# Retention and a GELU feed-forward on one core: the second batch by chunk, weight sums on VectorE, queries in token order, tails among other loads, and later chunks spread over seven blocks

## Chip, core and metric

One core of a Trainium2 chip. The metric is the device time of one execution in microseconds (us); the profile of one execution is taken on the chip beside the timed runs.

## What is computed

`q`, `k`, `v` are float32 of shape (8 batches, 8 heads, 576 tokens, 64). Each head has a decay; the attention has no softmax. Its output, laid out as 4608 tokens x 512, goes through a feed-forward with a tanh GELU.

```python
scores = scale * np.matmul(q, k.transpose(0, 1, 3, 2))
gamma = 1.0 - 2.0 ** (-5.0 - np.arange(H))
Dmat = np.where(rel >= 0, gamma[:, None, None] ** rel[None, :, :], 0.0)   # rel = query position - key position
attn = np.matmul(scores * Dmat, v)
x = attn.transpose(0, 2, 1, 3).reshape(4608, 512)
h = x @ w_in                                                             # 512 x 2048
out = gelu_tanh(h) @ w_out                                               # 2048 x 512
```

## The kernel before

*Attention.* A batch is cut into four chunks of 128 tokens (`c` = 0 to 3) and a tail of 64 (`c` = 4, called `NC`). The decay is split into factors on q and k, so that casting q and k from float32 to float16 also multiplies by a table `sc`. For each chunk:

- `cast` turns loaded float32 (`ld`, 16 buffers; `lt`, 3 buffers for tails) into `cq`, `ck`, `cv`;
- `turn_pe` and `turn_tail` transpose q and k on TensorE (PE) and copy the result to `tq` and `tk`; batches 4 to 7 use a DMA transpose instead (`turn_dma`, issued from ScalarE's queue);
- `score` multiplies keys by queries into two PSUM banks, and VectorE masks them (`ret`);
- `state` makes the chunk's 64x64 state, `scan` adds it to the running state on VectorE (`ws`) and spreads it into a block-diagonal tile (`tbd`);
- `av` makes the chunk's output from `ret`, v and the state of the chunk before, and `put` copies it from PSUM to `xT` on ScalarE (ACT). `xT` is a ring of 1536 tokens.

q is loaded in another order than k and v: a partition holds four neighbouring tokens, in pieces of 1 KB, where k and v come in pieces of 256 bytes. So `tq` and the scores have the tokens of a chunk in an interleaved order, and `put` undoes it with a strided write (`i j` to `j i`).

*Feed-forward.* Tokens go in nine tiles of 512; what runs for tile `t` is called block `t`. `up(t, fc)` makes one of 16 slices of h (four matmuls of 512 columns) and ACT applies the GELU into `gT`. Block 0's second product is plain (64 matmuls, two in each of 32 steps, with a store step behind each 16). Blocks 1 to 8 use a seven-product scheme with half-size operands: `act_sums` adds and subtracts quarters of `gT` on VectorE, `weight_sums` does so once for w_out, and `prod(t, m, u)` runs products m = 1, 6, 5, 7, 2, 3, 4 in two halves each; `after` combines the results and stores them. Such a block has 30 steps: 0 to 15 `up`, 16 to 29 `prod`.

*Order.* The order of work is written out by hand: `at(t, u, f)` hangs an attention piece on step u of block t, and engines work through their instructions in that order. Batch 0 runs first, beside the loads; up(0) follows with batch 0's tail between its slices (`late`); batch 1 hangs on block 0; batch b from 2 on hangs on block b-1, with five scores at steps 1, 7, 12, 19, 25 (6, 10, 15, 19, 25 for batch 2). Blocks 7 and 8 have no attention. POOL casts most q and k, ACT casts v.

All loads and stores are issued from SP, in one order, `seq`: batch 0 (q, then k and v by chunk, then tails), w_in, w_out, then batch by batch. `pump` issues the next load when a cast has freed an `ld` buffer.

Of the kernel before, what the change touches and what calls it, by code (L numbers as in the profile page):

```python
# [10 lines left out]
ALU = mybir.AluOpType  # L11
# [8 lines left out]
def kernel(  # L20
# [25 lines left out]
    QT = NC  # L46
    TB = 512
# [19 lines left out]
    def ldt():  # L67
        return sb.tile([128, 256], F32, tag="lt", name="lt", bufs=3)
# [4 lines left out]
    def load(b, key, c):  # L73
        src = SRC[key]
        if c == NC:
            t = ldt()
            for u in range(2):
                nc.sync.dma_start(  # L78
                    out=t[64 * u : 64 * u + 64, :].rearrange("p (h d) -> p h d", d=D),
                    in_=src[b, 4 * u : 4 * u + 4, M0:S, :].rearrange("h s d -> s h d"),  # L80
                )
        elif key == "q":
# [30 lines left out]
    for b in range(1, B):  # L113
        seq += [("b", b, "q", p) for p in range(HP)]
        seq += [("b", b, key, c) for c in range(NC) for key in "kv"]
        seq += [("b", b, key, NC) for key in "kqv"]
# [30 lines left out]
    NE = 8 + HP * 8 + 8  # L147
# [5 lines left out]
    for j in range(QT):  # L153
# [6 lines left out]
        )  # L160
    for u in range(2):
# [6 lines left out]
    nc.vector.tensor_scalar(out=sc[:, 8:44], in0=sc[:, 8:44], scalar1=scale, scalar2=None, op0=ALU.mult)  # L168
    warm = const.tile([128, 1], F32, name="warm")
# [6 lines left out]
    cm = const.tile([128, HP, QT, 32], F32, name="cm")  # L176
# [3 lines left out]
        pattern=[[0, HP], [1, QT], [QT, 32]], channel_multiplier=-1,  # L180
# [31 lines left out]
    def cast(b, key, c, eng):  # L212
# [9 lines left out]
        elif key == "q" and c < NC:  # L222
# [7 lines left out]
        else:  # L230
            s0, nh = (0, 8) if c < NC else ({"q": 40, "k": 44}[key], 4)
# [7 lines left out]
    def new_turned(b):  # L239
        a = att[b]  # L240
        for key in "kq":
            a["t" + key] = sb.tile([128, NB, 128], F16, tag="t" + key, name="t" + key, bufs=2)

    def turn_pe(b, key, c0, n, copy, tag="att"):
        a = att[b]
        t = bank(tag, "tr", F16)
        for i in range(n):
            nc.tensor.transpose(
                t[:, 128 * i : 128 * i + 128],
                a[key][:, 128 * (c0 + i) : 128 * (c0 + i) + 128],  # L250
                ident,
            )
# [463 lines left out]
```

## Time and profile before

| | |
|---|---|
| time, median of 3 runs | 345.28 us (344.16 to 345.38) |
| the profiled execution | 344.22 us; span 342.3 us from first to last instruction |
| busy, share of the span | PE 91%, DVE (VectorE) 62%, ACT 50%, POOL 32% |
| DMA | 51.30 MB, mean 150 GB/s |
| mean granted TensorE clock | 0.973 of full |

The span is cut into 40 equal slices. Each digit is the busy share of a slice in tenths; PEclk is the granted TensorE clock in tenths:

```profile
PE   5869849994697999999999999999999999999995
DVE  7751644879978467757976677467546752442432
ACT  3575516782455247525752673368326623613610
POOL 7748234999920460039224404100000000000000
PEclk9999969997889999999999999999999999999999
DMA  7979998989901999896986978410730003003003
```

One slice is 8.6 us. Batch 0 and up(0) take the first five, block 0 the next three and a half, block 1 the six behind those.

### The profile page before, as it was taken

Reading aid. Unit: us, or ns where it says so; the run is one execution under the profiler, and the core shown is the slowest. Engines: PE = TensorE matmul, PEld = TensorE weight load, DVE = VectorE, ACT = ScalarE, POOL = GpSimd, SP = SyncE. Lnnn points to the kernel's source line nnn. Section 1 sums busy time; section 2 is a strip of 40 time slices with the busy share of each in tenths; the row PEclk is TensorE's granted clock in tenths of the full one; section 3 lists DMA queues with packets and bytes.
Section 4 is the critical chain, followed back from the end, with each engine's and each line's share of the span. In section 5 each row is a group of like instructions: output and inputs, shape, how many; then the busy total and the mean of one; then the engine's idle time right before and its main releaser. Section 6 shows DMA issues by size and latency. Waiting matters only on the chain.

```text
span 342.3 us, 6651 instructions
## 1 busy us (share of the span) xinstructions
PE 310.2 (91%) x2660; PEld 189.1 (55%) x2660; DVE 213.1 (62%) x437; ACT 170.9 (50%) x274; POOL 108.8 (32%) x129
## 2 busy tenths in 40 slices
PE   5869849994697999999999999999999999999995
PEld 2434324452246854784477448745864585486484
DVE  7751644879978467757976677467546752442432
ACT  3575516782455247525752673368326623613610
POOL 7748234999920460039224404100000000000000
PEclk9999969997889999999999999999999999999999
DMA  7979998989901999896986978410730003003003
GB/s 204 194 204 359 388 288 178 247 169 296 207 6 31 229 188 293 166 188 205 256 170 159 283 162 101 139 39 2 138 124 0 2 2 123 0 2 123 2 0 124
DMA packets 116559, 51.30 MB, mean 150 GB/s; under 512 B 99632, under 2 KB 107824, under 8 KB 116528
## 3 DMA queue, kind: packets, MB, share of 16 engines
q1 hardware_dynamic: 97840, 46.15, 52.0%
q10 hardware_dynamic: 18688, 4.72, 8.1%
q8 instruction: 21, 0.34, 0.4%
q14 instruction: 10, 0.08, 0.1%
HBM read 36.70 MB, written 9.44 MB: 135 GB/s over the span
## 4 chain that ended last, share of the span: by engine, by line
PE 72%; DMA 8%; DVE 8%; SPq 5%; ACT 4%; issue 1%; POOL 1%; DVEq 0%
PE hp L390 30%; PE opB L466 12%; PE opC L466 9%; PE opA L466 8%; PE op L408 3%; DMA ld<-in_moe_w_in_dram 3%; DMA ld<-in_moe_w_out_dram 3%; PE xs L338 3%; SPq L90 3%; PE st L289 2%; PE xs L356 2%; ACT xT L377 2%; PE us L309 2%; DMA ld<-in_q_dram 2%; SPq L78 1%
## 5 line engine op out<-in xcount | busy, mean ns | idle before, releaser
L390 PE MATMUL hp<-xT,w_in_sb 128*128 128x512 f16 x576 | 136.3, 387 | 2.1 <-ACT xT L377 1.9
L396 ACT ACTIVATE gT<-hp 128x512 f16<-128x512 f32 x144 | 86.5, 605 | 67.7 <-PE hp L390 67.7
L390 PEld LDWEIGHTS <-w_in_sb 128*128 128x128 f16 x576 | 54.7, 99 | 63.3 <-issue 6.8
L298 DVE TENSOR_TENSOR ret<-st,cm 128x512 f16<-128x512 f32 x64 | 41.2, 685 | 27.5 <-PE st L289 27.5
L377 ACT CAST xT<-xs 128x512 f16<-128x512 f32 x31 | 40.1, 1294 | 29.5 <-PE xs L356 22.6
L466 PEld LDWEIGHTS <-gT 128*128 128x128 f16 x512 | 49.1, 98 | 6.5 <-issue 0.7
L223 POOL TENSOR_TENSOR cq<-ld,sc 128x512 f16<-128x512 f32 x28 | 31.6, 1155 | 46.0 <-DMA tq<-cq 21.0
L232 POOL TENSOR_TENSOR ck<-ld,sc 128x512 f16<-128x512 f32 x27 | 28.9, 1089 | 37.3 <-PE us L309 29.6
L466 PEld LDWEIGHTS <-s 128*128 128x128 f16 x384 | 36.5, 98 | 4.9
L466 PE MATMUL opA<-w_out_sb,gT 128*128 128x256 f16 x256 | 30.9, 273 | 0.0
L448 DVE TENSOR_TENSOR s<-gT 128x512 f16<-128x512 f16 x32 | 15.0, 469 | 21.5 <-ACT gT L396 21.1
L480 DVE TENSOR_TENSOR k<-k,opB 128x512 f32<-128x512 f32 x16 | 11.0, 687 | 23.7 <-PE opB L466 23.6
L289 PE MATMUL st<-tq,tk 64*128 64x128 f16 x288 | 15.8, 226 | 9.3 <-DVE tk L254 8.6
L329 DVE CAST tbd<-ws 64x256 f16<-64x256 f32 x48 | 20.6, 430 | 1.2
L289 PEld LDWEIGHTS <-tk 64*128 64x128 f16 x288 | 8.5, 96 | 22.9 <-DVE tk L254 11.1
L338 PEld LDWEIGHTS <-cv 128*64 128x64 f16 x288 | 9.6, 110 | 16.3 <-issue 13.9
L408 PE MATMUL op<-w_out_sb,gT 128*128 128x512 f16 x64 | 17.7, 396 | 0.5 <-ACT ost L413 0.5
L219 ACT CAST cv<-ld 128x512 f16<-128x512 f32 x28 | 17.5, 628 | 1.1 <-DMA ld<-in_v_dram 1.1
L480 DVE TENSOR_TENSOR ost<-k,opC 128x512 f32<-128x512 f32 x16 | 11.0, 687 | 11.0 <-PE opC L466 10.8
L338 PE MATMUL xs<-ret,cv 128*64 128x128 f16 x288 | 16.1, 228 | 1.1 <-ACT xT L377 1.1
L466 PE MATMUL opB<-wt,gT 128*128 128x256 f16 x128 | 16.4, 273 | 0.5 <-DVE ost L480 0.5
L449 DVE TENSOR_TENSOR s<-s,gT 128x512 f16<-128x512 f16 x32 | 15.9, 498 | 1.1
(92 smaller groups left out, 338.9 us busy)
## 6 DMA issues: line engine op xcount, KB each, us to landing
out_dram<-ost SPq DMA_DIRECT2D x17, 512.0 KB, 3.1
ld<-in_q_dram SPq DMA_DIRECT2D x32, 256.0 KB, 4.7
ld<-in_k_dram SPq DMA_DIRECT2D x32, 256.0 KB, 5.7
ld<-in_v_dram SPq DMA_DIRECT2D x32, 256.0 KB, 5.1
ld<-in_moe_w_in_dram SPq DMA_DIRECT2D x16, 256.0 KB, 6.2
ld<-in_moe_w_out_dram SPq DMA_DIRECT2D x16, 256.0 KB, 5.4
lt<-in_k_dram SPq DMA_DIRECT2D x16, 64.0 KB, 3.8
lt<-in_q_dram SPq DMA_DIRECT2D x16, 64.0 KB, 2.9
```

Of the source, the lines that this page charges most:

```text
L223: eng.tensor_tensor(out=dst.rearrange("p (j l d) -> p l j d", j=QT, l=2), in0=raw.rearrange("p (l j d) -> p l j d", l=2, j=QT), in1=sc[:, ...
L232: eng.tensor_tensor(out=dst.rearrange("p (h d) -> p h d", d=D), in0=raw.rearrange("p (h d) -> p h d", d=D), in1=sc[:, s0 : s0 + nh].unsque ...
L289: nc.tensor.matmul(st[hl][:, 128 * p : 128 * p + 128], a["tk"][r, 4 * c + p, :], tq(b, r, c, p), start=True, stop=True,)
L298: nc.vector.tensor_tensor(out=r[:, 0:w], in0=st[hl][:, 0:w], in1=m, op=ALU.mult)
L329: cp(out=td[r, c, :, r], in_=w[r])
L338: nc.tensor.matmul(xs[64 * hl : 64 * hl + 64, 128 * p : 128 * p + 128], a["v"][:, col(c, p, hl)], a["ret"][c, hl][:, 128 * p : 128 * p + 128],
L377: nc.scalar.copy(out=xT[:, g0 : g0 + 2].rearrange("p g n (i j) -> p g n j i", j=QT), in_=src)
L390: nc.tensor.matmul(hp.rearrange("p (g t) -> p g t", t=TL), w_in_sb[:, ct, 128 * fc : 128 * fc + 128], xT[:, o : o + TB // TL, ct, :], star ...
L396: nc.scalar.activation(out=gT[t][:, fc].rearrange("p i n -> p (i n)"), in_=hp, func=AF.Gelu_apprx_tanh)
L408: nc.tensor.matmul(op[i], gT[t][:, f, i], w_out_sb[:, f, :], start=(f == 0), stop=(f == NF - 1))
L466: nc.tensor.matmul(op[tag][:, HD * u : HD * u + HD], lhs(f), rhs[:, f], start=(new and u == 0 and f == 0), stop=(f == NH - 1), skip_group_ ...
L480: nc.vector.tensor_tensor(out=o, in0=a, in1=b, op=ALU.add)
```

## The change

- *Second batch by chunk.* Batch 1's four chunks hang on steps 16, 20, 24, 28 of block 0 (turn), 2 steps later score, state and scan, with the output of the chunk before; batch 1's tail goes to block 1. Batch 0's tail moves from up(0) to block 0: its casts to step 0, `turn` 3, `score` 6, `av` 9, `put` 10. Batch 1's queries are turned at steps 12 and 14 instead of 2 and 4.
- *Weight sums on VectorE.* The POOL operations over float32 intermediates become four float16 operations on VectorE for each half of the slices (step 33 of block 0, step 2 of block 1), into four tiles; `weight_copy` on ACT goes.
- *Queries in token order.* Queries of batches 2 to 7 are loaded like keys. For batches 0 and 1 the copy behind the transpose (`turn_q4`) puts the tokens in order. The masks and `put` use plain order.
- *Tails among other loads.* A tail is loaded in two pieces placed between other loads; `lt` has 4 buffers. Batch 0's come between w_out loads.
- *Later chunks over blocks 1 to 7.* Batch 1's tail and the 30 chunks and tails of batches 2 to 7 follow a `plan` of four or five per block.
- Besides: the w_out casts all stand at slices 11 to 14 of up(0); keys of batches 1 and 2 are cast on POOL; the spread into `tbd` is a function of its own and always on ACT, two steps after the scan; the DMA transposes are issued from SP; `act_sums` works on halves of four slices instead of four times two.

The core of the diff:

```diff
-    seq = [("b", 0, "q", p) for p in range(HP)]
-    seq += [("b", 0, key, c) for c in range(NC) for key in "kv"]
-    seq += [("b", 0, key, NC) for key in "kqv"]
-    seq += [("i", g, ct) for g in range(4) for ct in range(4)]
-    seq += [("o", f) for f in range(NF)]
...
+    def body(b):
+        if b < NQ:
+            return [("b", b, "q", p) for p in range(HP)] + [("b", b, key, c) for c in range(NC) for key in "kv"]
+        return [("b", b, key, c) for c in range(NC) for key in "kqv"]
+
+    def mixed(loads, b):
+        pieces = [("b", b, key, NC, u) for key in "kqv" for u in range(2)]
+        n = len(loads) // len(pieces)
+        out = []
+        for i, x in enumerate(loads):
+            out.append(x)
+            if i % n == n - 1 and pieces:
+                out.append(pieces.pop(0))
+        return out
+
+    seq = body(0) + [("i", g, ct) for g in range(4) for ct in range(4)]
+    seq += mixed([("o", f) for f in range(NF)], 0)
+    seq += body(1) + mixed(body(2)[:6], 1) + mixed(body(2)[6:], 2)
+    for b in range(3, B):
+        seq += mixed(body(b), b)
...
+    def turn_q4(b, p0, copy, tag="att"):
...
+        copy(
+            out=a["tq"][:, 4 * p0 : 4 * p0 + 8, :].rearrange("p (n c) t -> p n (c t)", n=2)
+            .rearrange("p n (i j) -> p n j i", j=QT),
+            in_=t.rearrange("p (n j i) -> p n j i", n=2, j=QT),
+        )
...
-            nc.scalar.dma_start_transpose(out=a["t" + key], in_=a[key])
+            nc.sync.dma_start_transpose(out=a["t" + key], in_=a[key])
...
-        src = xs.rearrange("p (n j g i) -> p g n j i", n=HP, j=QT, g=2)
+        src = xs.rearrange("p (n g t) -> p g n t", n=HP, g=2)
         if g0 + 1 < NG:
-            nc.scalar.copy(out=xT[:, g0 : g0 + 2].rearrange("p g n (i j) -> p g n j i", j=QT), in_=src)
+            nc.scalar.copy(out=xT[:, g0 : g0 + 2], in_=src)
...
     def weight_sums(f):
-        s = slice(f, f + 2)
-        d, w = (sb.tile([128, 2, HD], F32, tag=n, name=n, bufs=b) for n, b in (("wd", 2), ("we", 1)))
-        nc.vector.tensor_tensor(out=wt["1"][:, s], in0=W12[:, s], in1=W11[:, s], op=ALU.subtract)
-        nc.gpsimd.tensor_tensor(out=d, in0=W22[:, s], in1=W12[:, s], op=ALU.subtract)
...
+        s = slice(f, f + 4)
+        for o, x, y, f in (
+            ("1", W12, W11, ALU.subtract), ("3", W22, W12, ALU.subtract),
+            ("2", wt["3"], W11, ALU.add), ("4", W21, wt["2"], ALU.subtract),
+        ):
+            nc.vector.tensor_tensor(out=wt[o][:, s], in0=x[:, s], in1=y[:, s], op=f)
...
+    at(0, -12, lambda: nc.gpsimd.memset(tbd[1], 0.0))
+    for f in range(NF):
+        at(0, -5 + f // 4, lambda f=f: cast_w("o", f))
+    at(0, 0, lambda: [cc(0, key, NC, e) for key, e in zip("kqv", (V, P, P))])
+    at(0, 3, lambda: turn(0, NC, V.tensor_copy))
+    at(0, 6, lambda: score(0, NC))
+    at(0, 9, lambda: av(0, NC))
+    at(0, 10, lambda: put(0, NC))
...
     for p, e in enumerate((V, P, V, P)):
+        at(0, 2 + p, lambda p=p, e=e: cc(1, "q", p, e))
+    at(0, 12, lambda: turn_q4(1, 0, A.copy))
+    at(0, 14, lambda: turn_q4(1, 2, V.tensor_copy))
+    for c in range(NC):
+        u = 16 + 4 * c
+        at(0, u, lambda c=c: (cc(1, "k", c, P), cc(1, "v", c, P), turn(1, c, A.copy)))
+        if c:
+            at(0, u, lambda c=c: spread(1, c - 1, A.copy))
+        at(0, u + 2, lambda c=c: (score(1, c, "hp"), state(1, c), scan(1, c)))
+        if c:
+            at(0, u + 2, lambda c=c: (av(1, c - 1), put(1, c - 1)))
+    at(0, 33, lambda: (av(1, 3), put(1, 3), spread(1, 3, A.copy), weight_sums(0)))
+    at(1, 2, lambda: weight_sums(4))
...
+            at(t0, ut[-1] + 1, lambda b=b: tail_casts(b, (P, P, A)))
         if b >= NPE:
+            at(t0, ut[-1] + 2, lambda b=b: turn_dma(b))
+
+    todo = [(1, NC)] + [(b, c) for b in range(2, B) for c in CH]
+    plan = {1: (12, 17, 20, 24), 2: (2, 6, 12, 18, 23), 3: (2, 7, 12, 20), 4: (1, 6, 11, 17, 23),
+            5: (2, 7, 12, 20), 6: (1, 6, 11, 17, 23), 7: (2, 7, 12, 20)}
+    for t, us in plan.items():
+        for u in us:
+            b, c = todo.pop(0)
             if b < NPE:
+                at(t, u - (3 if (t, u) == (1, 17) else 2), lambda b=b, c=c: turn(b, c, V.tensor_copy))
+            at(t, u, lambda b=b, c=c: score(b, c))
             if c < NC:
+                at(t, u, lambda b=b, c=c: (state(b, c), scan(b, c)))
+                at(t, u + 2, lambda b=b, c=c: spread(b, c, A.copy))
+            at(t, u + 3, lambda b=b, c=c: av(b, c))
+            at(t, u + 4, lambda b=b, c=c: put(b, c))
...
-                    if f in (2, 4, 6):
-                        act_sums(t, f - 2, f)
+                    if f == 4:
+                        act_sums(t, 0, 4)
                     if f == 7:
-                        act_sums(t, 6, 8)
+                        act_sums(t, 4, 8)
```

For batches from 4 on, casts hang on steps 16 to 23 of block b-2, the tail's on step 24 and the DMA transposes on step 25.

More of the change, by code (lines that the diff above doesn't have):

```diff
@@ L221, in cast @@
                 eng.tensor_copy(out=dst, in_=raw)
-        elif key == "q" and c < NC:
+        elif key == "q" and c < NC and b < NQ:
             eng.tensor_tensor(
@@ L546 @@
     filler(8)
[L547 to L549 removed]
+    turn_q4(0, 0, A.copy, "A")
+    turn_q4(0, 2, V.tensor_copy, "B")
+    turn(0, 0, A.copy)
     for c in range(NC):
@@ L555 @@
             cc(0, "v", c + 1, P)
-            turn_pe(0, "k", 4 * c + 4, 4, A.copy)
+            turn(0, c + 1, A.copy)
         else:
-            for key, e in zip("kqv", (P, P, P)):
-                cc(0, key, NC, e)
             for g in range(4):
@@ L562 @@
                     cast_w("i", g, ct)
-        scan(0, c, A.copy)
+        scan(0, c)
+        spread(0, c, A.copy)
         filler(3)
@@ L566 @@
         put(0, c)
-    late = {
-        0: lambda: turn_tail(0, V.tensor_copy),
-        2: lambda: score(0, NC),
-        4: lambda: av(0, NC),
-        5: lambda: put(0, NC),
-    }
     events = {}
```

187 lines of the change are left out of this document (64 added, 123 removed).

## The prediction

> **What bounds the kernel now.** I read the chain of waits first, then the busy times of single stretches.
>
> ```profile
> PE 72%; DMA 8%; DVE 8%; SPq 5%; ACT 4%; issue 1%; POOL 1%; DVEq 0%
> ```
>
> TensorE carries 72% of the chain; the rest must lie in some stage. The next rows cut the span: block 1 (steps of token tile 1), block 3, block 7, and three short stretches. Columns: window, length, busy time of PE, PEld, DVE, ACT and POOL with instruction counts, granted clock, DMA share, GB/s.
>
> ```profile
> 71.50:121.00 49.50, 39.59 (x353) 24.48 (x350) 39.50 (x64) 22.94 (x39) 29.83 (x27) 0.90 0.66 153
> 154.70:187.50 32.80, 32.12 (x298) 20.32 (x296) 25.35 (x46) 17.70 (x28) 15.84 (x17) 1.00 0.85 195
> 285.90:312.00 26.10, 26.10 (x178) 17.22 (x176) 9.52 (x21) 10.72 (x18) 0.00 (x0) 1.00 0.09 35
> 47.00:51.00 4.00, 3.39 (x19) 2.03 (x20) 0.89 (x1) 1.08 (x2) 3.16 (x3) 0.50 1.17 222
> 83.50:89.00 5.50, 5.48 (x28) 2.23 (x28) 5.39 (x7) 1.19 (x2) 5.42 (x6) 0.54 1.09 244
> 94.00:99.00 5.00, 5.00 (x32) 1.94 (x34) 4.48 (x11) 1.70 (x3) 2.03 (x3) 0.66 0.06 13
> ```
>
> Block 7 is feed-forward alone: 26.1 us, PE never idle. Block 3 adds one batch of attention: 32.8 us, PE idle 0.7. Those stages are PE's. Block 1 takes 49.5 us, idle for 9.9 and partly at half clock: the profile's real hole. The chain (start, length, what) gives block starts and the end.
>
> ```profile
> 71.62 2.63 PE hp L390 x12
> 121.07 0.86 PE hp L390 x4
> ...
> 337.71 1.05 PE opB L466 x8
> ```
>
> Block 0 ends near 71.4, block 1 at 121.07, PE's work at 338.76. Behind that lie 3.6 us to the span's end (342.3), and 1.9 from there to the profiled execution's 344.22; that run is 1.1 us below the median of 345.28. Now the front, from the timeline (start, length, engine; idle time before in brackets):
>
> ```profile
> 12.71 1.72 SPq L78 DMA_DIRECT2D lt<-in_k_dram  x2
> 17.11 12.19 SPq L100 DMA_DIRECT2D ld<-in_moe_w_in_dram  x16
> 40.44 1.46 PE L408 MATMUL op<-w_out_sb,gT 128*128 128x512 f16 x6
> 45.56 0.43 DVE L522 CAST w_out_sb<-ld 128x512 f16<-128x512 f32 x1 [0.27 <-DMA ld<-in_moe_w_out_dram]
> 46.31 0.69 DVE L223 TENSOR_TENSOR cq<-ld,sc 128x512 f16<-128x512 f32 x1 [0.32 <-DMA ld<-in_q_dram]
> 47.05 0.61 PE L248 MATMUL tr<-ident,cq 128*128 128x128 f16 x4 [5.16 <-DVE cq L223]
> 50.33 0.93 PE L248 MATMUL tr<-ident,cq 128*128 128x128 f16 x8
> ```
>
> Block 0 starts at 40.44, then PE idles 5.16 us because step 2 wants batch 1's queries, which are loaded behind w_out. The last w_out cast starts at 45.56, the first query cast at 46.31; step 4's transposes end at 51.3.
>
> **The change, part by part.** *Loads.* Batch 0's six tail DMAs held SP from 12.71 to 17.11, 4.4 us; now they sit between w_out loads. All bytes ahead of the last w_out block are the same, so it can come earlier only by DMA time that is idle now.
>
> ```profile
> 10.00:15.00 5.00, 4.32 (x44) 2.42 (x43) 3.08 (x5) 2.19 (x5) 3.71 (x5) 1.00 1.10 219
> 15.00:20.00 5.00, 4.67 (x64) 2.69 (x60) 3.83 (x8) 4.05 (x6) 2.95 (x4) 1.00 0.61 148
> 20.00:25.00 5.00, 2.59 (x42) 1.53 (x37) 2.46 (x5) 4.15 (x7) 2.49 (x4) 1.00 0.85 214
> ```
>
> Against a full share of 1.10, these hold (0.49 + 0.25)/1.10 x 5 = 3.4 us. The other estimate is 4.4 us less the tails' own bytes, 0.39 MB at about 200 GB/s = 2.0: 2.4 us. Bounds 0 and 4.4; I take 2.8: the last w_out cast ends at 45.99 - 2.8 = 43.2.
>
> *Block 0's new gate.* The 16 w_out casts stand on VectorE ahead of the cast of batch 0's key tail (V at step 0), and the tail is now turned on PE at step 3. VectorE is in order, so PE waits at step 3 for the last w_out block, not for queries. Rows that price this and the other pieces, from the groups by shape (busy us, mean ns):
>
> ```profile
> L232 DVE TENSOR_TENSOR ck<-lt,sc 128x256 f16<-128x256 f32 x2 | 1.4, 718 | 0.0
> L254 DVE COPY tq<-tr 128x1024 f16<-128x1024 f16 x6 | 4.1, 678 | 4.2 <-PE tr L248 4.2
> L377 ACT CAST xT<-xs 128x512 f16<-128x512 f32 x31 | 40.1, 1294 | 29.5 <-PE xs L356 22.6 <-POOL ck L232 6.4 <-PE xs L338 0.2
> L370 ACT CAST xT<-xs 128x256 f16<-128x256 f32 x8 | 3.0, 372 | 16.8 <-PE xs L348 16.7
> L380 ACT CAST xT<-xs 128x256 f16<-128x256 f32 x2 | 1.3, 781 | 0.0
> ```
>
> Gate: 43.2 + 0.72 + 0.1 = 44.0 us. Until then PE has only up(0) and steps 0 to 3 (1.7 us); up(0) ends at 40.44 now, and not later after, since batch 0's tail leaves it, w_in comes earlier and its puts are shorter. So the start may shift by some us without moving the gate; the extra scale constants (two tiny VectorE operations) and the slower reordering copies of batch 0's queries (at least 0.68 us each, at most 1.3 with L380's twofold) are covered by that. Step 12, which turns batch 1's queries, comes 4 us or more behind the gate, when they have landed: the first is cast 0.75 us behind the last w_out now. PE will have idled some 4 to 6 us, so its clock drops: the three stretches above ran 4.0, 5.1 and 3.4 us at half clock (length x (1 - clock) x 2), a mean loss of 2.1 us. The Trainium skill (TensorE: Matmul & The Clock Gate, Part 1) says that one busy window of about 3.4 us restores the clock; that would lose 1.7 us, and the sum would be 0.4 lower.
>
> What follows the gate is PE's own work, priced from the chain:
>
> ```profile
> 52.78 1.29 PE op L408 x6
> ...
> 128.47 0.22 PE tr L248 x4
> ...
> 129.56 0.33 PE st L289 x8
> 129.88 0.24 PE us L309 x8
> ...
> 132.83 0.34 PE xs L338 x8
> 133.17 0.33 PE xs L356 x4
> ...
> 135.00 1.19 ACT xT L377
> ...
> 150.44 0.22 PE st L289 x4
> ...
> 153.39 0.23 PE xs L338 x4
> 153.62 0.22 PE xs L348 x4
> ```
>
> A step of block 0 is 2 x 0.215 = 0.43. A chunk is 0.33 + 0.24 + 0.34 + 0.33 = 1.24 (the first of a batch 0.91), a tail 0.67, four transposes 0.22. From the gate: 30 steps 12.9; batch 0's tail 0.7; 16 query transposes 0.9; batch 1's four chunks with key transposes 0.9 + 4.6 = 5.5; half clock 2.1; other waits 1.2, which is what the same arithmetic leaves over now between 51.3 and 71.4 (20.1 against 18.9). Block 0 ends at 44.0 + 23.3 = 67.3, now 71.4. Batch 1's keys and values do not bind: 0.52 MB a chunk take 2.4 us at the 222 GB/s of 47 to 51 us and two POOL casts 2.2, while PE needs 3.2 for four steps and a chunk.
>
> *Block 1.* Two things go: POOL's 16 weight-sum operations, in front of which batch 2's casts queued, and two of five chunks (steps 12, 17, 20, 24 hold batch 1's tail and three chunks of batch 2). PE: 26.1 + 0.9 (tail and its transposes) + three chunks 3.4 + 24 transposes 1.3 = 31.7. What is late next is VectorE: eight sums of 128x1024 at the start, then four activation sums, then the tail's copy that step 12 needs.
>
> ```profile
> L429 DVE TENSOR_TENSOR wt<-w_out_sb x4: 416/990/1281, 70.9 to 83.4; 128x512 f16<-128x512 f16 x4
> ```
>
> Undisturbed 0.42 for 512 elements; beside POOL up to 1.28. No row has 1024: bounds 0.42 and 2.56. Undisturbed I take 0.7, near L254's 0.68. POOL's operations (29.83 us for 27 in block 1's row, 1.1 each) are paced by loads, two to a chunk's 4 to 5 us, so about half the sums collide, for 0.4 us on average: 1.1 each. VectorE: 66.5 + 8.8 = 75.3, four activation sums 79.7, copy 80.2; PE arrives at step 12 near 79. So a wait of about 1; two chunks three steps apart (17, 20) share PSUM banks, 0.5 more. Block 1: 33.2, end 100.5.
>
> *Blocks 2 to 8.* Now 338.76 - 121.07 = 217.7. To it come batch 2's last chunk and tail with transposes (1.24 + 0.67 + 0.66 = 2.6) and batch 3's query transposes (0.9), done in block 1 today. The spreading over block 7 only moves PE work: free in itself. The put in token order writes 64-element runs, as L370 does: 256 elements in 0.37 against 0.78 strided (L380), so 512 should take about 0.6 for 1.29. PE's wait for it goes:
>
> ```profile
> PE us L309 <- ACT xT L377: 2.5, 4, 0.7
> PE us L309 <- ACT xT L380: 0.7, 1, 0.7
> ```
>
> That is 3.2 us of blocks 2 to 8, all in the slot where put stands one step ahead of the next score. New slots 4 and 5 steps apart, and activation sums in halves (the second half is ready near 1.4 us after the last gelu; product 1 covers 1.75), cost something: bounds 0 and about 5 (0.7 for each of seven blocks); I take 1.5. The state's spread moves to ACT, which is busy 17.7 us of block 3's 32.8. Queries in 256-byte pieces make their loads cost what keys cost; the DMA share in block 3 is 0.85, and block 7's is 0.09. The transposes by DMA move from ACT's queue to SP's, behind the last casts at step 25:
>
> ```profile
> tk<-ck ACTq DMA_TRANSPOSE x4, 4.9
> tq<-cq ACTq DMA_TRANSPOSE x4, 6.4
> ```
>
> 11.3 us in series; the first use (batch 4, step 12 of block 3) is about 17 us later. Behind them on SP stand the loads of a batch needed a block later and two stores, whose buffers are wanted 25 steps on: hidden. Sum: 217.7 + 3.5 - 3.2 + 1.5 = 219.5, PE's end at 320.0, span 323.6, profiled time 325.5. With the median slightly above a profiled run, 326.
>
> **The rivals.** *VectorE blocks block 1.* If POOL is nearly always in a cast, a sum costs 2.0 (twice L429's median of 0.99), VectorE is done with weights at 82.5 and activations at 90.5, and PE stalls 11.5 us at step 12, of which 1 is charged, and loses 2.1 more to the clock; a half-way case adds 3 and 2. For it: 83.50 to 89.00, DVE and POOL both full. Against: POOL's weight sums, which filled it then, are gone. 331 to 338.5. The Trainium skill (SBUF — State Buffer, Who interferes with whom) has a VectorE instruction with two SBUF inputs contend with a GpSimd one that reads SBUF, the loser blocked for a whole instruction. That is this rival at its end, a full cast of 1.1 on each of twelve operations; L429's 1.28 against 0.42 agrees where POOL is full.
>
> *No gate.* The last w_out comes by the full 4.4 us, the clock stays, and the waits that I charge (1.2, 1.5, 1.5) do not appear: 326 - 1.6 - 2.1 - 4.2 = 318. For it: block 7's zero idle. Against: DMA shares near 1.
>
> *Put stays at 1.29*, PSUM's reading being the cost: the 3.2 stays and slots 4 or 5 steps apart add some 0.5 each in twelve places: 335. L380 against L370 speaks against.
>
> *Slower: SP's queue.* If DMA transposes on SP land late, PE waits at the first score of each of batches 4 to 7, and its clock drops. Four such waits of x + 2.1 eat the gain of 19 from x = 2.7; at x = 4 the time is 350. For batch 4 the landing must be some 8.5 us late, for the others 14 or more. For it: loads and stores on SP share the queue. Against: issue to landing at 4.9 and 6.4, and PE's only waits on put and copies in these blocks.
>
> **How the numbers follow.** Forecast 0.57 (its own range 321 to 331), VectorE 0.20, no gate 0.12, put 0.05, SP's queue 0.04, no net change through several smaller losses 0.02. Range 316 to 337: from below the no-gate case to near the worst VectorE one. Half a per cent, 1.7 us, is what a measurement of this kernel can tell from none. Faster 0.94, same 0.02, slower 0.04.
>
> **What would show it.** In the changed profile: the put near 0.6 us; a PE idle of 4 to 6 us ahead of four transposes of batch 0's tail in block 0, ended by VectorE's k cast near 44, then a clock of 0.5 for 4 us; block 0's end near 67 and block 1's near 100; no PE wait above 3 us behind that; blocks 3 to 7 between 31 and 33. I am wrong if the PE idle sits elsewhere: at step 12 of block 1 (VectorE), or at a score of batches 4 to 7 (SP).

## The result, and the profile after

The changed kernel's median is 336.39 us (four executions, 333.69 to 339.04) against 344.73 for the kernel before beside it: ratio 0.9731, 95% interval 0.9667 to 0.9796. Five later executions gave 334.64 (333.42 to 335.17), ratio 0.9718 [0.9687, 0.9748]. The forecast of 326.0 had the sign right and less than half of the promised 19 us came. Below, kernels are compared by their ratios to the kernel before, because they ran on different chips; 0.001 of ratio is 0.34 us, and "the changed kernel" stands for 0.972. Medians are of all executions, while ratios leave out those more than 1.5% above the fastest of their kernel, such as the 339.04 above and one of 393.67, at a mean granted clock of 0.761, of the kernel called "no gate, quarters" below.

The profiled execution took 333.69 us, with a span of 332.0. Its chain of waits, the share by engine, and those entries of the chain that begin block 1, begin block 2 and end TensorE's work:

```profile
PE 69%; DVE 12%; DMA 9%; SPq 4%; ACT 4%; issue 1%; POOL 0%; DVEq 0%
```

```profile
68.55 1.90 PE hp L403 x8
...
104.94 0.86 PE hp L403 x4
...
327.34 1.05 PE opB L472 x8
```

TensorE's share of the chain fell from 72% to 69% and VectorE's rose from 8% to 12%: the kernel is shorter, but it is not the TensorE-bound kernel of the forecast. Against that forecast, in the same profiled execution: block 0 ends at 68.55 for 67.3 (+1.2), block 1 takes 36.4 for 33.2 (+3.2), blocks 2 to 8 take 223.45 (104.94 to 328.39) for 219.5 (+4.0). These 8.4 us are the whole miss of the profiled execution; the 3.6 us behind TensorE's end and the 1.7 outside the span came nearly as charged (3.6 and 1.9). The median adds some 2 us: it lies 2.7 above the profiled execution, where I had charged 0.5.

The same windows as before, by the new times (columns as before: PE, PEld, DVE, ACT, POOL, clock, DMA share, GB/s); the rows are the 5 us of the new gate and block 1:

```profile
45.00:50.00 5.00, 4.06 (x18) 1.68 (x19) 3.46 (x7) 0.00 (x0) 2.82 (x3) 0.66 1.11 253
68.55:104.94 36.39, 32.96 (x297) 21.33 (x297) 25.55 (x37) 20.74 (x41) 16.80 (x16) 1.00 1.11 210
```

Block 1 idles for 3.4 us of TensorE instead of 9.9, and no longer loses the clock. Where TensorE still waits, from the waits of TensorE over the whole run (total, times, longest):

```profile
PE tr L276 <- DVE ck L245: 4.3, 1, 4.3
PE st L302 <- DVE tt L280: 3.5, 3, 1.8
...
PE us L321 <- DVE ret L308: 1.6, 2, 0.8
...
PE tr L276 <- DVE ret L308: 1.2, 1, 1.2
```

The first is the gate that the prediction announced. The second and its relatives are VectorE, late with copies of transposes and with masks. The kernel before had such waits too, all in block 1 (its copies stand at L254):

```profile
PE st L289 <- DVE tk L254: 8.6, 3, 4.7
```

What is new is that two of the three, 1.8 and 1.0 us, lie in block 2. Behind block 1 TensorE waits for nothing but VectorE. My reading is that VectorE is late because its activation sums and GpSimd's casts slow each other down. These are the timelines in block 2: GpSimd's casts, VectorE's sums and the copy behind them, and TensorE's scores that wait for that copy and for the one behind the second half of the sums:

```profile
114.64 1.04 POOL L245 TENSOR_TENSOR ck<-ld,sc 128x512 f16<-128x512 f32 x1
115.64 1.49 POOL L245 TENSOR_TENSOR cq<-ld,sc 128x512 f16<-128x512 f32 x1
...
114.86 1.36 DVE L454 TENSOR_TENSOR s<-gT 128x1024 f16<-128x1024 f16 x1 [0.84 <-ACT gT L409]
116.26 1.42 DVE L455 TENSOR_TENSOR s<-s,gT 128x1024 f16<-128x1024 f16 x1
117.60 1.52 DVE L456 TENSOR_TENSOR gT<-gT 128x1024 f16<-128x1024 f16 x1
119.05 1.52 DVE L457 TENSOR_TENSOR s<-gT,s 128x1024 f16<-128x1024 f16 x1
120.50 0.68 DVE L280 COPY tt<-tr 128x1024 f16<-128x1024 f16 x1
...
121.23 0.40 PE L302 MATMUL st<-tt 64*128 64x128 f16 x8 [1.81 <-DVE tt L280]
129.12 0.40 PE L302 MATMUL st<-tt 64*128 64x128 f16 x8 [1.03 <-DVE tt L280]
```

A cast takes 1.04 us alone and 1.49 here; a sum takes 1.4 to 1.5 here. How long a sum takes alone is what one of the experiments shows.

### The profile page after: what moved, and what is told of

Its sections match the earlier page's. It is cut to its first block, busy times and chain, and to the rows that moved or that the text cites. A ratio compares the mean times of both kernels' runs of the same rounds, so it can differ in the third digit from the quotient of the medians.

```text
span 332.0 us, 6557 instructions
## 1 busy us (share of the span) xinstructions
PE 305.7 (92%) x2660; PEld 187.4 (56%) x2660; DVE 193.2 (58%) x320; ACT 167.8 (51%) x312; POOL 102.7 (31%) x122
## 4 chain that ended last, share of the span: by engine, by line
PE 69%; DVE 12%; DMA 9%; SPq 4%; ACT 4%; issue 1%; POOL 0%; DVEq 0%
PE hp L403 26%; PE opB L472 12%; PE opC L472 9%; PE opA L472 7%; DMA ld<-in_moe_w_out_dram 5%; PE op L421 4%; DMA ld<-in_moe_w_in_dram 4%; PE st L302 3%; PE xs L351 3%; SPq L90 3%; DVE s L455 2%; DVE s L457 2%; DVE s L454 2%; DVE gT L456 2%; PE us L321 2%; PE xs L369 2%
## 5 line engine op out<-in xcount | busy, mean ns | idle before, releaser
L403 PE MATMUL hp<-xT,w_in_sb 128*128 128x512 f16 x576 | 132.8, 380 | 2.0 <-ACT xT L390 2.0
L245 POOL TENSOR_TENSOR ck<-ld,sc 128x512 f16<-128x512 f32 x31 | 36.1, 1166 | 99.4 <-issue 44.3
L342 ACT CAST tbd<-ws 64x256 f16<-64x256 f32 x64 | 25.8, 403 | 18.5 <-DVE ws L337 17.7
L472 PE MATMUL opB<-wt,gT 128*128 128x256 f16 x256 | 30.9, 273 | 0.5 <-DVE ost L486 0.5
L454 DVE TENSOR_TENSOR s<-gT 128x1024 f16<-128x1024 f16 x16 | 14.1, 883 | 26.0 <-ACT gT L409 26.0
L302 PE MATMUL st<-tt 64*128 64x128 f16 x288 | 15.6, 224 | 5.8 <-DVE tt L280 3.5
L390 ACT CAST xT<-xs 128x512 f16<-128x512 f32 x31 | 18.1, 582 | 3.5 <-PE xs L369 2.4
L302 PEld LDWEIGHTS <-tt 64*128 64x128 f16 x288 | 8.4, 96 | 19.8 <-issue 10.7
L504 ACT COPY ost<-opA 128x512 f32<-128x512 f32 x8 | 4.7, 585 | 23.5 <-PE opA L472 23.5
L472 PE MATMUL opC<-wt,s 128*128 128x256 f16 x128 | 16.3, 273 | 0.0
```

The costliest lines, as they stand in the source:

```text
L245: eng.tensor_tensor(out=dst.rearrange("p (h d) -> p h d", d=D), in0=raw.rearrange("p (h d) -> p h d", d=D), in1=sc[:, s0 : s0 + nh].unsque ...
L302: nc.tensor.matmul(st[hl][:, 128 * p : 128 * p + 128], a["tk"][r, 4 * c + p, :], tq(b, c, p)[r], start=True, stop=True)
L342: cp(out=tbd[b % 2][r, c, :, r], in_=att[b]["w"][r])
L390: nc.scalar.copy(out=xT[:, g0 : g0 + 2], in_=src)
L403: nc.tensor.matmul(hp.rearrange("p (g t) -> p g t", t=TL), w_in_sb[:, ct, 128 * fc : 128 * fc + 128], xT[:, o : o + TB // TL, ct, :], star ...
L454: nc.vector.tensor_tensor(out=s["1"], in0=a21, in1=a22, op=ALU.add)
```

## The experiments

Lengths of blocks in us, each from the start of its first `up` product in the timeline, and TensorE's end, one profile for each kernel:

| kernel | block 0 ends | block 1 | 2 | 3 | 4 | 5 | 6 | 7 | TensorE's end | median | ratio [interval] |
|---|---|---|---|---|---|---|---|---|---|---|---|
| changed | 68.55 | 36.2 | 37.0 | 31.6 | 33.1 | 31.8 | 32.1 | 31.1 | 328.4 | 336.4 | 0.9731 [0.9667, 0.9796] |
| changed, again | 68.79 | 35.9 | 38.1 | 31.6 | 33.1 | 31.7 | 32.1 | 31.1 | 329.3 | 334.6 | 0.9718 [0.9687, 0.9748] |
| no gate | 66.86 | 36.2 | 38.6 | 31.6 | 33.1 | 31.8 | 32.1 | 31.1 | 328.2 | 330.7 | 0.9606 [0.9576, 0.9636] |
| casts late | 67.31 | 38.8 | 40.3 | 32.5 | 36.1 | 31.3 | 32.1 | 31.1 | 336.5 | 341.4 | 0.9905 [0.9869, 0.9940] |
| quarters | 67.87 | 36.2 | 35.6 | 31.3 | 32.1 | 32.0 | 32.1 | 31.0 | 325.0 | 329.9 | 0.9581 [0.9550, 0.9612] |
| pairs | 68.43 | 38.7 | 38.2 | 31.6 | 33.1 | 31.7 | 32.1 | 31.1 | 331.9 | 333.8 | 0.9671 [0.9636, 0.9706] |
| casts light | 68.92 | 35.3 | 35.1 | 31.6 | 32.1 | 30.7 | 32.1 | 31.1 | 323.9 | 329.0 | 0.9542 [0.9504, 0.9580] |
| weight sums back | 70.92 | 39.6 | 37.0 | 31.6 | 33.1 | 31.7 | 32.1 | 31.1 | 334.1 | 339.2 | 0.9822 [0.9778, 0.9867] |
| put twice | 66.64 | 36.1 | 37.0 | 32.3 | 33.1 | 32.1 | 33.3 | 32.3 | 329.8 | 336.0 | 0.9757 [0.9700, 0.9815] |
| not spread | 67.91 | 36.4 | 37.0 | 33.0 | 32.0 | 32.0 | 32.0 | 28.3 | 325.6 | 331.6 | 0.9652 [0.9614, 0.9690] |
| tails first | 68.67 | 37.2 | 37.0 | 31.6 | 33.1 | 31.7 | 32.1 | 31.1 | 329.4 | 335.4 | 0.9713 [0.9661, 0.9766] |
| no gate, quarters, pairs | 66.49 | 35.5 | 35.6 | 31.3 | 32.1 | 32.0 | 32.1 | 31.0 | 323.0 | 327.5 | 0.9496 [0.9445, 0.9547] |
| no gate, quarters | 64.17 | 35.3 | 35.6 | 31.3 | 32.1 | 32.0 | 32.1 | 31.0 | 320.4 | 327.3 | 0.9508 [0.9469, 0.9547] |
| no gate, quarters, not spread | 65.57 | 35.0 | 35.6 | 32.7 | 32.0 | 32.0 | 32.0 | 28.2 | 320.0 | 327.1 | 0.9526 [0.9488, 0.9564] |

A block ends where the next one begins. In the profile of the kernel with pairs the granted clock fell to 0.66 from 90 to 95 us and to 0.69 from 125 to 130; its blocks 1 and 2 aren't compared.

The theory after the result: the gate costs some 4 us in block 0, and GpSimd's bursts of casts meet VectorE's activation sums in blocks 1, 2, 4 and 5. Rivals: the activation sums are too large a lump by themselves; the put; GpSimd's casts as such; the loads.

**No gate.** Batch 0's tail is cast on GpSimd, so that nothing of it stands behind the w_out casts on VectorE.

```diff
-    at(0, 0, lambda: [cc(0, key, NC, e) for key, e in zip("kqv", (V, P, P))])
-    at(0, 3, lambda: turn(0, NC, V.tensor_copy))
-    at(0, 9, lambda: av(0, NC))
-    at(0, 10, lambda: put(0, NC))
+    at(0, 0, lambda: [cc(0, key, NC, e) for key, e in zip("kqv", (P, P, P))])
+    at(0, 3, lambda: turn(0, NC, A.copy))
+    at(0, 14, lambda: av(0, NC))
+    at(0, 15, lambda: put(0, NC))
```

> Batch 0's key tail is cast on POOL instead of VectorE, its transposes are copied by ACT, and its av and put stand at steps 14 and 15. If VectorE's order is what holds PE at step 3 of block 0 (idle 4.3 us before, ended by the k cast at 45.9), that idle goes, the next wait is at step 12 for batch 1's queries (about 2 us), the half clock of block 0 (3.6 us) mostly goes, and block 0 ends near 65 us for 68.5: 3 to 4 us less. If the loads alone set that stage, the wait only moves to step 12 and grows there to 4 us, and the time stays within 1 us.

Median 330.73, ratio 0.9606: 4 us less than the changed kernel. The timeline shows the gate gone and what is late next, batch 1's queries:

```profile
45.90 0.43 DVE L528 CAST w_out_sb<-ld 128x512 f16<-128x512 f32 x1 [0.59 <-DMA ld<-in_moe_w_out_dram]
47.45 0.40 PE L261 MATMUL tr<-ident,cq 128*128 128x128 f16 x4 [1.35 <-DVE cq L236]
48.59 0.61 PE L261 MATMUL tr<-ident,cq 128*128 128x128 f16 x4 [0.75 <-POOL cq L236]
```

One wait of 4.3 becomes two of 1.35 and 0.75. Against my expectation the clock still dropped: it was 0.86 from 45 to 50 us and 0.80 from 50 to 55, and 1.7 us were lost, as in the changed kernel. The profile holds 1.7 to 1.9 us of the gain (block 0's end). It is the slowest of the six executions, 333.53, and lost 1.6 us of block 2 to the clock; the rest of the median's gain lies in executions that were not profiled.

**Casts late.** From batch 3 on, GpSimd first copies eight values of the last GELU's output, so that its burst cannot start before the GELUs are done.

```diff
+            at(t0, 16, lambda t0=t0: nc.gpsimd.tensor_copy(out=gsc, in_=gT[t0][:, NF - 1, 0, 0:8]))
         at(t0, ut[0], lambda b=b: (new_casts(b), new_turned(b)))
```

> POOL's casts for batches 3 to 7 wait for the last GELU of their block (a tiny POOL copy that reads it stands ahead of them), so that their bursts of 8 to 10 casts run beside the products and not beside the activation sums. Theory VectorE against POOL: the sums (1.4 to 1.5 us each in blocks 2, 4 and 5) go back to 0.69, block 2 from 37.0 to about 34, blocks 4 and 5 to about 31.5 and 30.3: 5 to 6 us less. Theory order alone (halves of four slices are too long in VectorE's queue, POOL or not): no block changes by more than 0.5. Theory loads late: slower, since casts free the buffers later.

341.42, ratio 0.9905: it lost 6 us, and of the three theories only the last (loads late) had the sign. The first half of the activation sums came down to 0.68 and 0.69 each, but the burst and the second half wait for the same GELU and start together:

```profile
126.01 1.04 POOL L246 TENSOR_TENSOR ck<-ld,sc 128x512 f16<-128x512 f32 x1
126.03 1.56 DVE L456 TENSOR_TENSOR s<-s,gT 128x1024 f16<-128x1024 f16 x1
```

There products wait for the sums at once, TensorE waits 2.9 for the copy behind them, the granted clock falls to 0.50 from 130 to 135 us, and the late casts delay the DMA transposes behind them in SP's queue: TensorE waits for one, 2.3 us, the SP rival's mechanism. So the run doesn't decide for a remedy, but it shows that the collision goes where the burst goes.

**Quarters.** The activation sums go back to four times two slices, as before the change.

```diff
-                    if f == 4:
-                        act_sums(t, 0, 4)
+                    if f in (2, 4, 6):
+                        act_sums(t, f - 2, f)
                     if f == 7:
-                        act_sums(t, 4, 8)
+                        act_sums(t, 6, 8)
```

> The activation sums in four pieces of two slices as in the kernel before, all else as after. Theory VectorE against POOL: twelve to sixteen short operations each wait for a POOL cast, so a colliding stage gets longer on VectorE (about 16 x 1.1 for 8 x 1.45 us), but it starts earlier and PE's waits stay: within 2 us of the changed kernel, rather slower. Theory order alone: the waits of blocks 2, 4 and 5 go, 4 to 5 us less.

329.94, ratio 0.9581: 5 us less. This is the figure of the theory of order alone; mine, within 2 us, failed. Block 2 is 1.4 shorter, block 4 by 1.0. The collisions are still there, in smaller pieces: a sum of 512 elements, the mask that gets in behind the first four, and TensorE's score.

```profile
112.34 1.26 DVE L456 TENSOR_TENSOR gT<-gT 128x512 f16<-128x512 f16 x1
...
114.71 0.74 DVE L308 TENSOR_TENSOR ret<-st,tm 128x256 f16<-128x256 f32 x2
...
120.17 0.40 PE L302 MATMUL st<-tt 64*128 64x128 f16 x8 [1.14 <-DVE tt L280]
```

The first four sums start before the last GELUs of their half, so that the copy behind all eight ends sooner and the score waits 1.14 instead of 1.81. The second wait of block 2 (1.03) is gone. By itself this run does not part the size of the sums from their meeting with casts.

**Casts light.** This kernel leaves out most of batches 3 to 7's attention: their k and q casts become a fill and a multiplication of 16 columns.

```diff
+            if b >= 3:
+                eng.memset(dst, 0.01)
+                eng.tensor_tensor(out=dst[:, 0:16], in0=raw[:, 0:16], in1=sc[:, 0:16], op=ALU.mult)
+                return
```

> For batches 3 to 7 POOL casts q and k only in 16 of 512 columns and fills the rest by a memset, which reads no SBUF: those batches' attention is left out in the main, all waits and transfers stay. The activation sums keep their halves. Theory VectorE against POOL: no sum takes above 0.9 us from block 2 on, the 3 us wait of block 2 and the 1.6 us of blocks 4 and 5 go, 5 to 6 us of the span and up to 3 more of the clock's drops: 327 to 331. Theory halves in VectorE's order alone: 334 to 336, sums of 0.69 already too long a piece.

328.97, ratio 0.9542: 6 us less. The same four sums and the copy:

```profile
114.26 0.69 DVE L458 TENSOR_TENSOR s<-gT 128x1024 f16<-128x1024 f16 x1 [0.85 <-ACT gT L413]
114.98 0.69 DVE L459 TENSOR_TENSOR s<-s,gT 128x1024 f16<-128x1024 f16 x1
115.59 0.74 DVE L460 TENSOR_TENSOR gT<-gT 128x1024 f16<-128x1024 f16 x1
116.26 0.68 DVE L461 TENSOR_TENSOR s<-gT,s 128x1024 f16<-128x1024 f16 x1
117.12 0.69 DVE L284 COPY tt<-tr 128x1024 f16<-128x1024 f16 x1 [0.18 <-PE tr L280]
```

The sums take 2.8 us in all instead of 5.8, with halves kept: it is the meeting with casts that makes them long, and the score behind that copy no longer waits. Size has a share of its own. Behind the second half of the sums, at 0.69 each, the wait stays, and only quarters remove it:

```profile
126.63 0.40 PE L306 MATMUL st<-tt 64*128 64x128 f16 x8 [1.03 <-DVE tt L284]
```

From block 2's start in the chain (104.34) to TensorE's end (323.88) it takes 219.5 us, the forecast's figure: the 4 us missed there are this collision, 1.9 in block 2 and about 1 each in blocks 4 and 5. Block 3's sums meet casts as well (1.41 to 1.53 for three of the first four in the changed kernel), but no score or product waits there, and it stays at 31.6. In block 1 light casts take 1.0 off; 2 remain.

**Weight sums back on GpSimd** (three of the four operations, in slices of two, f16).

```diff
+        for s in (slice(f, f + 2), slice(f + 2, f + 4)):
+            nc.vector.tensor_tensor(out=wt["1"][:, s], in0=W12[:, s], in1=W11[:, s], op=ALU.subtract)
+            for o, x, y, e in (
+                ("3", W22, W12, ALU.subtract), ("2", wt["3"], W11, ALU.add), ("4", W21, wt["2"], ALU.subtract),
+            ):
+                nc.gpsimd.tensor_tensor(out=wt[o][:, s], in0=x[:, s], in1=y[:, s], op=e)
```

> The weight sums of the changed kernel on POOL again (all but wt1, in pieces of two slices, twelve POOL operations of about 1.3 us), all else as after. If moving them to VectorE was what freed block 1, batch 2's casts come up to 15 us later, PE waits at the first chunks of batch 2 and the time is 5 to 10 us more. If the later slots of batch 2 and the loads cover it (batch 2's casts wait for loads anyway), it stays within 2 us.

339.24, ratio 0.9822: 3.5 us more, between the two expectations. Block 1 is 3.4 longer, about 1.7 of it at a lower clock (0.83 from 90 to 100 us) behind new waits. (Its block 0 ends 2.4 late: its last w_out cast began at 46.55, and the clock lost 3.4 us from 45 to 55 instead of 1.7; the edit touches neither the loads nor that wait.) So this part of the change gains about 3 us, with intervals that leave 1.6 to 5.4.

**Put twice** (the copy to `xT` is issued twice from batch 2 on).

```diff
+            if b >= 2:
+                nc.scalar.copy(out=xT[:, g0 : g0 + 2], in_=src)
             nc.scalar.copy(out=xT[:, g0 : g0 + 2], in_=src)
```

> Every put of batches 2 to 7 that is one copy is done twice, 1.2 us of ACT as before the change. If the shorter put is worth what the prediction gave it (3.2 us of waits in old slots, 0.5 in each of the new ones four or five steps apart), this is 3 to 6 us slower than the changed kernel; if the new slots hide it, under 1 us.

336.02, ratio 0.9757, 1.3 us above the changed kernel and inside the intervals. Its blocks 3 to 7 are 3.4 longer, and the old wait returns:

```profile
PE us L321 <- ACT xT L392: 3.5, 6, 0.6
```

So the trace agrees with the price of the put (3.2 charged); the median shows 1.3 of it, between the two expectations. Block 0 ended 1.9 earlier in its profile, which the edit doesn't touch; that offset is why a single profile's end or a median of four isn't enough for 3 us here.

**Pairs** (batch 0's six tail pieces come two at a time between the w_out loads).

```diff
-            if i % n == n - 1 and pieces:
-                out.append(pieces.pop(0))
+            if i % (2 * n) == 2 * n - 1 and pieces and b == 0:
+                out += [pieces.pop(0), pieces.pop(0)]
+            elif b and i % n == n - 1 and pieces:
+                out.append(pieces.pop(0))
```

> Batch 0's six tail pieces (64 partitions each) stand in three adjacent pairs between w_out loads instead of singly. If a single piece costs 0.67 us of the queue because it fills only half of the DMA engines (a pair of w_out loads with a piece takes 2.05 us, without 1.38), adjacent halves overlap: the last w_out cast ends near 43.6 for 45.55, PE's wait at step 3 is 2 us shorter, and the time falls by 1 to 2 us. If the small pieces cost their bytes however they stand, nothing moves by more than 0.5.

333.82, ratio 0.9671. The last w_out cast starts at 44.80, within what unchanged loads give (43.6 to 46.6). Together with two edits above, no gate and quarters, it gave 327.54:

> Three edits together: batch 0's key tail off VectorE (as in the run without the gate), activation sums in quarters, and tail pieces in pairs. If each removes a wait of its own, their gains add: 336 - 5.7 - 6.5 - 2 = 322; if the first and the third free the same wait (both the gate in block 0), 324 to 326.

That is above both figures: the gains don't add up. Those two edits without the pairing gave 327.25, so it does nothing that can be seen:

> Two edits together: batch 0's tail casts on GpSimd instead of behind the w_out casts on VectorE (no gate at step 3 of block 0), and activation sums in quarters; w_out's loads as changed. Nothing is left out. With the tail pieces paired as well this gave 327.5. Theory (the pairing did nothing): 327.5 +- 1.2. Rival (pairing brings w_out earlier, since two pieces in a row cost the queue less than one twice): 329 or more, with the last w_out cast a microsecond later than 44.76.

In that last kernel TensorE carries 78% of the chain of waits and VectorE 18%; its last w_out cast starts at 43.62. It beats the kernel before by 17 us and the changed one by 7. Block 0 ends 4.4 earlier than in the changed kernel, blocks 2 to 8 are 2.7 shorter.

**Tails first.** Batch 0's tails are loaded ahead of w_in again.

```diff
-    seq = body(0) + [("i", g, ct) for g in range(4) for ct in range(4)]
-    seq += mixed([("o", f) for f in range(NF)], 0)
+    seq = body(0) + [("b", 0, key, NC, u) for key in "kqv" for u in range(2)]
+    seq += [("i", g, ct) for g in range(4) for ct in range(4)]
+    seq += [("o", f) for f in range(NF)]
```

> Undoes one part: batch 0's tail pieces are loaded ahead of w_in again, and w_out's loads stand without pieces between them; everything else is as changed. Nothing is left out. Theory (moving the tails brought nothing to the gate, since what w_in gains w_out loses to the mixed loads): the last w_out cast starts at 45.1 +- 1.4, block 0 ends at 68.5 +- 1.5, time within 1.5 us of the changed kernel. The prediction's own term (the last w_out comes 2.8 us earlier by this move): the cast starts near 48, block 0 ends near 71.3, time 2.8 us longer.

335.35, ratio 0.9713, the changed kernel's own. The last w_out cast starts at 45.05 (in the mixed order 45.12 and, repeated, 43.90):

```profile
45.05 0.43 DVE L529 CAST w_out_sb<-ld 128x512 f16<-128x512 f32 x1 [1.49 <-DMA ld<-in_moe_w_out_dram]
```

The load of that last cast landed 1.49 us behind the cast before, so its start alone doesn't settle the matter. The medians do: the 2.8 us of the forecast would be 0.008 of ratio, and the two differ by 0.0005, give or take 0.006. No gain of the moved tails can be seen.

**Not spread.** Five chunks in blocks 3 and 5, two in block 7.

```diff
-    plan = {1: (12, 17, 20, 24), 2: (2, 6, 12, 18, 23), 3: (2, 7, 12, 20), 4: (1, 6, 11, 17, 23),
-            5: (2, 7, 12, 20), 6: (1, 6, 11, 17, 23), 7: (2, 7, 12, 20)}
+    plan = {1: (12, 17, 20, 24), 2: (2, 6, 12, 18, 23), 3: (2, 7, 12, 18, 23), 4: (1, 6, 11, 17, 23),
+            5: (1, 6, 11, 17, 23), 6: (1, 6, 11, 17, 23), 7: (2, 7)}
```

> Undoes the spreading of late chunks alone: blocks 3 and 5 get five chunks instead of four, block 7 two instead of four; nothing is left out. Theory (blocks 3 to 7 are TensorE's, so moving a chunk moves its 1.24 us and nothing else): within 1.5 us of the changed kernel; blocks 3 and 5 longer by 1.2 to 1.9 each, block 7 shorter by 2.5 to 3.5. Rival (chunks four or five steps apart run out of PSUM banks and of VectorE, so that spreading was worth something): slower by 2 us or more than the changed kernel, with new waits of TensorE on VectorE's masks or on puts in blocks 3 and 5.

331.64, ratio 0.9652: 2.3 us less, which neither theory had. Block 3 got longer by one chunk (1.4), block 7 shorter by two (2.7), as charged. But block 4, whose plan is untouched, got 1.0 shorter, and block 5 took one chunk more for 0.3. The cause is when GpSimd's burst starts. Changed kernel, then this one: the state (`us`) of the last chunk of batch 4, the first cast of batch 6 into the buffer that it frees, and the first activation sum.

```profile
181.25 0.32 PE L321 MATMUL us<-cv,ck 128*64 128x64 f16 x8
181.70 1.04 POOL L245 TENSOR_TENSOR ck<-ld,sc 128x512 f16<-128x512 f32 x1 [21.55 <-issue]
183.95 1.53 DVE L454 TENSOR_TENSOR s<-gT 128x1024 f16<-128x1024 f16 x1
```

```profile
176.38 0.32 PE L321 MATMUL us<-cv,ck 128*64 128x64 f16 x8
176.83 1.04 POOL L245 TENSOR_TENSOR ck<-ld,sc 128x512 f16<-128x512 f32 x1 [17.19 <-DMA ld<-in_v_dram]
183.64 0.97 DVE L454 TENSOR_TENSOR s<-gT 128x1024 f16<-128x1024 f16 x1 [0.84 <-ACT gT L409]
```

Spreading moved that last chunk from step 1 to step 6 of block 4, and so the burst of ten casts by 5 us, into the sums: the four take 6.0 us there and 4.6 here. Block 5 shows the same (6.0 and 4.6). If so, this gain and that of the quarters are one and the same. The run with both edits:

> Three edits together: batch 0's tail casts on GpSimd (no gate at step 3 of block 0), activation sums in quarters, and late chunks not spread over blocks 3, 5 and 7 as in the run of five chunks a block. Nothing is left out. Quarter sums alone gave 31.33, 32.05, 31.96, 32.09 and 31.00 us for blocks 3 to 7 (158.4), the plan alone 157.3 against the changed kernel's 159.6. Theory (the plan helped only because it moves the state that frees GpSimd's cast buffers from step 6 to step 1, so that the burst of casts ends before the activation sums; the quarters relieve the same collision): blocks 3 to 7 sum to 157.3 +- 0.5, so the gain over the two edits without the plan is 0.6 to 1.6 us, not 3; 326 us. Rival (the plan saves something of its own, a PSUM bank or a tail in block 7): the full 2.2 to 3 us are saved again, 324.5 or less, blocks 3 to 7 at 156.2 or less.

327.10, ratio 0.9526. Blocks 3 to 7 sum to 156.9 against 158.4 with quarters alone: 1.5 us, not the full 2.2 to 3, and block 4 gains 1.0 once, not twice. In the median nothing is left of it (327.10 and 327.25). The 1.5 lies in block 5, which takes its extra chunk for nothing: with quarters alone TensorE still waits there 1.05 us for a sum, and with the plan too it doesn't. Both edits relieve the same collision, then, in block 4 the same part of it; the three best kernels can't be told apart.

**The changed kernel again.**

> The changed kernel itself, once more, beside the other runs of this call. Theory (the last three microseconds between the profiled 333.7 and the median of 336.4 are clock drops that come and go): the median lies at 336 +- 1.5 again, its executions spread over 333 to 338 with granted clocks between 0.98 and 0.995, and the longer ones have the lower clocks: 1.7 us of spread for each 0.005 of mean clock. Rival (the spread has nothing to do with the clock, but with when the loads land): time and clock are unrelated over the executions. If the last w_out cast moves by more than 1 us against the first profile (45.12), the front is not the same from one execution to the next.

The median, 334.64, is at the low edge. Time and clock go together, but not at that price: the execution at 0.994 took 333.42, three at 0.974 took 334.07 to 334.92, one at 0.969 took 335.17: 1.75 us for 0.025 of clock, a fifth of what I expected. The granted clock of its page shows why. Of the 8.7 us that the mean of 0.974 stands for, 3.4 lie in the second slice, where loads set the pace: w_in's begin at 12.57, and at 12.53 in the first profile, where the clock of that slice was full. Another 3.4 lie at the gate, in the sixth slice and behind it, but here the gate opened 1.2 us sooner.

```profile
PEclk9599969999999989999999999999999999999999
```

What shows in the time is the drop near 120 us, behind block 2's wait of 1.81 for VectorE: 38.1 us for block 2, instead of 37.0 in the first profile, where the same wait was followed by full clock.

```profile
120.00:125.00 5.00, 3.90 (x26) 1.72 (x27) 2.66 (x5) 0.99 (x2) 1.48 (x2) 0.74 1.11 306
```

## Why the prediction was wrong, step by step

*Loads: the step "I take 2.8" failed.* The last w_out cast started 0.4 us earlier (45.12 for 45.56), not 2.8. The move did what it says: w_in's loads begin at 12.53 instead of 17.11. But w_out's loads then run between tail pieces and are slower. The 10 us from 30 to 40 in windows, the kernel before first, then the changed one:

```profile
30.00:35.00 5.00, 5.00 (x31) 2.23 (x29) 0.00 (x0) 3.48 (x7) 4.56 (x9) 1.00 1.02 364
35.00:40.00 5.00, 5.00 (x24) 2.25 (x23) 4.17 (x7) 3.40 (x7) 1.76 (x2) 1.00 1.05 388
```

```profile
30.00:35.00 5.00, 5.00 (x25) 2.27 (x24) 2.96 (x5) 3.40 (x7) 2.26 (x2) 1.00 1.06 279
35.00:40.00 5.00, 5.00 (x25) 2.29 (x24) 2.08 (x5) 3.40 (x7) 0.61 (x1) 1.00 1.06 275
```

DMA is as busy in both (1.02 to 1.06) and moves a quarter less. My bounds counted idle time and the tails' bytes at their old rate; they didn't ask what the tails cost their new neighbours. The lower bound, 0, was near the answer, and the run with tails first agrees.

*The gate was right, in place and kind.*

```profile
45.12 0.43 DVE L528 CAST w_out_sb<-ld 128x512 f16<-128x512 f32 x1 [0.29 <-DMA ld<-in_moe_w_out_dram]
45.46 0.42 DVE L245 TENSOR_TENSOR ck<-lt,sc 128x256 f16<-128x256 f32 x1
45.94 0.39 PE L276 MATMUL tr<-ident,ck 128*128 128x128 f16 x2 [4.32 <-DVE ck L245]
```

It opened at 45.94 for 44.0: the loads came 2.4 late, and the cast of the tail took 0.42 for the 0.72 charged. From there block 0 took 22.6 us for 23.3. The half clock lost 5 x (1 - 0.66) = 1.7 us, not my 2.1. That is the estimate that the prediction worked out from the window of about 3.4 us in the Trainium skill (TensorE: Matmul & The Clock Gate, Part 1). In the repeated run the clock lost (0.89, 0.50, 0.93 in the three stretches of 5 us from 40 to 55) up to 3.4, so one window is not what every execution pays.

*Block 1: a wait at step 12 was right, "0.5 for banks" was too little, one wait was missing, and "31.7" was too little work.* TensorE's waits there are 1.6 for banks (`us` on `ret`, slots 20 and 24), 1.2 for a mask behind the second half of the sums, 0.6 for the copy at step 12: 3.4 where 1.5 was charged. (Another 0.7, for `xT`, stands just ahead of the block and counts to block 0.) The light casts took away the second (1.2 to 0.2). The other 1.3 of the 3.2 us is TensorE's own work, 32.96 busy for the 31.7 added up; chunks moved at 1.36 in a later experiment, for the 1.24 of the sum, which explains a part. The sums on VectorE themselves were no worse than the 1.1 each that I took: the eight weight sums have means of 0.68 to 1.05.

*Blocks 2 to 8: the term "I take 1.5" failed.* Its two sources, slots 4 and 5 steps apart and sums in halves, were the right places to look; with the 4.0 that the casts add it would have had to be 5.5, just outside its bounds of 0 and about 5. "The second half is ready near 1.4 us after the last gelu" counted sums at 0.7 each. Beside casts they take twice that. I had priced that collision for block 1 and confined the VectorE rival to it, though GpSimd casts the next batches in blocks 2 to 5 as well. That rival (331 to 338.5) named the engine and the mechanism; its place, step 12 of block 1, was wrong, so that 336.4 lies in its range is luck. Its price, a full cast of 1.1 on each operation, was too high: 0.7 to 0.85 us each.

*"The spreading only moves PE work: free in itself" failed.* A chunk moves at 1.36 us as TensorE's work, but its place also decides when a cast buffer comes free, and so where the burst falls: the run without spreading is 2.3 us faster.

*Right:* the put (582 ns mean for 0.6, and `us` no longer waits for it), and the DMA transposes on SP, hidden in the changed kernel. The reordering copies of batch 0 and 1's queries were bounded too low, 0.68 to 1.3. The prediction's own row of the old put (L377), with the same stride of four elements, would have priced them: 1.29 for 512, so 2.6 for 1024.

```profile
L390 ACT CAST xT<-xs 128x512 f16<-128x512 f32 x31 | 18.1, 582 | 3.5 <-PE xs L369 2.4 <-PE xs L351 0.8
L262 ACT COPY tt<-tr 128x1024 f16<-128x1024 f16 x2 | 4.9, 2448 | 2.4 <-PE tr L261 2.4
```

*Still open:* why the last w_out cast lands anywhere from 43.6 to 46.6 with the same order of loads, how much of a median's difference that is, and what put the first median 2.7 above its profile.

## What to carry to other kernels

When an engine is off the critical path, ask when its work starts, not only how much it is: here ten casts begin the moment one matmul frees a buffer, and moving that matmul by five steps moved them into another engine's sums. A price for two engines in each other's way, once found, belongs in every stage where both work, not only in the stage under study. A moved load is paid for by its new neighbours too, so compare bytes per second there, not idle time.

## What the runs showed of the hardware

When VectorE's sums (0.69 us alone) meet GpSimd's casts (1.04 alone), they take 1.36 to 1.53 and 1.49, and one of each is done in 1.45 to 1.5 us: more than the longer one alone, somewhat less than their sum of 1.73. The Trainium skill (SBUF — State Buffer, Who interferes with whom) has the loser of such a pair blocked for a whole instruction; here a sum loses 0.67 to 0.84 us and a cast 0.45, each less than the other's length. With light casts, GpSimd's fills, which read nothing, stayed at 0.53 us beside the sums, and its 16-column multiplications grew from 0.22 to 0.64 and 0.68 us, about one sum. Writing order sets the price of a copy: the put of 512 elements took 1.29 us with a stride of four elements and takes 0.58 in runs of 64, and the reordering copy of 1024 takes 2.45 us on ScalarE with that stride, where the kernel before had one in order at 1.01 (L254). The same wait of TensorE, 1.81 us in block 2, was followed by full clock in the first profile of the changed kernel and by 0.50 for two of the next five us in the second.
